# Narrowing spread over 19 units, late products moved, and a straight last block in an attention-and-SwiGLU kernel

## Chip, cores and metric

One core of one Trainium2 chip. The metric is the device time of one execution, in microseconds; the kernel before takes about 323.4. "Span" is the time from the first to the last instruction of a profiled execution; it is some 1.7 us shorter than the device time.

## The reference

```python
# attention: q, k, v are (4, 4, 1088, 32); S1, S2 are (8, 32)
def phi(x):                                        # 8 x 8 = 64 features
    a = einsum('rd,bhsd->bhsr', S1, x); b = einsum('rd,bhsd->bhsr', S2, x)
    return einsum('bhsi,bhsj->bhsij', a, b).reshape(..., 64)
kv = einsum('bhsf,bhsd->bhfd', phi(k), v);  z = sum(phi(k), axis=2)
attn = (phi(q) @ kv) / (phi(q) . z + 1e-6)
x = attn.transpose(0, 2, 1, 3).reshape(4352, 128)
# SwiGLU: w_gate, w_val (128, 1536), w_out (1536, 128)
g = x @ w_gate
out = (g * sigmoid(g) * (x @ w_val)) @ w_out
```

All inputs arrive as float64. The kernel reads them as pairs of 32-bit words and makes fp32 of them on the chip: this is the "narrowing".

## The kernel before: what the change and the argument touch

Tokens stand in 12 blocks (three per batch: 384, 384, 320), d_ff in 12 chunks of 128. One **unit** is a block and a chunk: a gate product and a value product on TensorE into two PSUM banks, silu on ScalarE, a product on VectorE. A **down** product accumulates the hidden tile times w_out. While the first batch's units run, the weights are still being narrowed, piece by piece (3 chunks, 384 columns), in three parts with a `yield` between them:

```python
def narrow(dst, raw, shape):
    ...
    # part one, VectorE: exponent field, mantissa field
    nc.vector.tensor_scalar(e[:], hi, 0x7FF00000, None, op0=ALU.bitwise_and)
    nc.vector.tensor_scalar(m[:], hi, 0xFFFFF, 0x100000, op0=ALU.bitwise_and, op1=ALU.bitwise_or)
    yield
    # part two, ScalarE: rebias, scale
    nc.scalar.activation(e[:], e[:], AF.Relu, bias=rebias[: shape[0], :], scale=8.0)
    nc.scalar.activation(f, m[:], AF.Copy, scale=2.0**-20)
    yield
    # part three, VectorE (two SBUF inputs each), then GpSimd
    nc.vector.scalar_tensor_tensor(out=e[:], in0=hi, scalar=-(1 << 31), in1=e[:], op0=ALU.bitwise_and, op1=ALU.bitwise_or)
    nc.vector.scalar_tensor_tensor(out=f, in0=lo, scalar=2.0**-52, in1=f, op0=ALU.mult, op1=ALU.add)
    mul = nc.vector if first else nc.gpsimd
    mul.tensor_tensor(out=dst, in0=f, in1=e[:].bitcast(FP32), op=ALU.mult)
    if not first:
        load_next()
    yield

def unit(i, j, late=False):
    g, u = bank(), bank()                      # banks in turn, four of them
    ...                                        # two matmuls, then silu into sg
    if late:                                   # six early units: VectorE has no time
        nc.scalar.copy(hj[:, 0:n], u[:, 0:n])
        lates.append((hj[:, 0:n], sg[:, 0:n]))
    else:
        nc.vector.tensor_tensor(out=hj[:, 0:n], in0=sg[:, 0:n], in1=u[:, 0:n], op=ALU.mult)

def catch_up():                                # the late product
    o, sg = lates.pop(0)
    nc.gpsimd.tensor_tensor(out=o, in0=o, in1=sg, op=ALU.mult)
...
parts = {0: both(3, *w), 1: both(3, *w), 2: both(3, "wg"), 4: both(3, "wv"),
         6: both(4, *w), 7: both(4, *w), 8: both(4, "wg"), 10: both(4, "wv"),
         12: [("wo", 0), ("wo", 1)], 13: [("wo", 0), ("wo", 1), ("wo", 2)], ...}
for z, (i, j) in enumerate(seq):               # units 0, 1, 2, ... of this stage
    unit(i, j)
    for p in parts.get(z, ()):
        part(*p)
    if z in (4, 10, 16, 24, 25, 26):
        catch_up()
    ...
    if z >= 17:
        down()
```

A block's result is transposed by VectorE and stored by four stores, one per 32 output columns. The very last block (320 tokens) uses two queues.

## Time and profile before

| | us |
|---|---|
| device time, median of 3 | 323.42 |
| span of the profile | 321.45 |
| unit 0's first gate product, first down product | 28.06, 52.91 |
| stage between them | 24.85 |
| end of the last matmul; from there to the end ("tail") | 316.98; 4.47 |

The numbers in rows of the timeline are start and length in us. The first 28 us load inputs and do the first batch's attention.

### The profile page before, as it was taken

How to read it: one execution, taken by the hardware profiler on the slowest of the kernel's cores; microseconds unless marked ns; L12 is line 12 of the kernel's file. 1: busy time of each engine (PE TensorE's matmuls, PEld its weight loads, DVE VectorE, ACT ScalarE, POOL GpSimd, SP SyncE). 2: the span in 40 equal slices, each digit the busy share in tenths (PEclk: the TensorE clock that was granted, in tenths of full speed). 3: DMA queues.
4: the chain of work that ended last, by engine and by line, in shares of the span. 5: the costliest groups of instructions: out<-in, count | busy, mean ns of one | idle time of the engine just before them, and what ended most of it. 6: DMA issues, size and time to landing. Idle time of an engine off the chain costs nothing.

```text
span 321.5 us, 5554 instructions
## 1 busy us (share of the span) xinstructions
PE 312.6 (97%) x2276; PEld 189.9 (59%) x2276; DVE 156.7 (49%) x330; ACT 99.0 (31%) x227; POOL 37.6 (12%) x53
## 2 busy tenths in 40 slices
PE   8889999999999999999999999999999999999994
PEld 6545555656556665555666656555667655556672
DVE  4887888653466522544643543354544332322331
ACT  3467555322121222322322322323222222222220
POOL 2322333173000140000000060000000000000000
PEclk9999999999999999999999999999999999999998
DMA  7543580204041201100210100000010100100101
GB/s 203 156 150 100 157 248 0 71 0 96 1 96 22 69 17 55 27 0 2 31 65 0 22 2 0 14 12 2 0 27 0 20 0 2 26 0 0 24 2 20
DMA packets 25017, 13.99 MB, mean 44 GB/s; under 512 B 18848, under 2 KB 23072, under 8 KB 24992
## 3 DMA queue, kind: packets, MB, share of 16 engines
q1 hardware_dynamic: 24304, 13.56, 16.5%
q8 instruction: 18, 0.29, 0.4%
q10 hardware_dynamic: 688, 0.08, 0.2%
q14 instruction: 7, 0.06, 0.1%
HBM read 11.41 MB, written 2.23 MB: 42 GB/s over the span
## 4 chain that ended last, share of the span: by engine, by line
PE 89%; DVE 5%; ACT 2%; issue 1%; DMA 1%; POOL 0%; DVEq 0%
PE bank L511 50%; PE bank L539 28%; PE a L348 2%; PE a L398 2%; PE b L348 1%; PE bank L194 1%; PE a L304 1%; ACT exp L221 1%; DVE exp L216 1%; DMA raw<-in_moe_w_out_dram 1%; PE b L398 1%; PE a L273 1%; PE b L327 1%; PE bank L316 1%; ACT man L222 0%
## 5 line engine op out<-in xcount | busy, mean ns | idle before, releaser
L525 DVE TENSOR_TENSOR hj<-sg,bank 128x384 f32<-128x384 f32 (+1 forms) x138 | 72.7, 529 | 122.6 <-PE bank L511 117.8
L517 ACT ACTIVATE sg<-bank 128x384 f32<-128x384 f32 (+1 forms) x144 | 67.8, 473 | 167.1 <-PE bank L511 165.5
L511 PE MATMUL bank<-xT,wg 128*128 128x384 f32 (+1 forms) x288 | 114.1, 478 | 2.3 <-POOL wg L232 1.1
L511 PE MATMUL bank<-xT,wv 128*128 128x384 f32 (+1 forms) x288 | 111.9, 470 | 0.3 <-DVE hj L525 0.3
L539 PE MATMUL bank<-hj,wo 128*128 128x384 f32 (+1 forms) x288 | 109.1, 471 | 0.1
L511 PEld LDWEIGHTS bank<-xT,wv 128*128 128x128 f32 x288 | 54.0, 190 | 35.2 <-DVE hj L525 3.6
L511 PEld LDWEIGHTS bank<-xT,wg 128*128 128x128 f32 x288 | 52.5, 190 | 36.8 <-issue 3.9
L539 PEld LDWEIGHTS bank<-hj,wo 128*128 128x128 f32 x288 | 54.0, 190 | 33.0 <-issue 2.4
L445 POOL TENSOR_TENSOR zs<-phk 128x1024 f32<-128x1024 f32 x3 | 7.1, 2352 | 107.1 <-PE bank L511 106.0
L376 DVE TENSOR_TENSOR phq<-a,qb 128x384 f32<-128x384 f32 (+1 forms) x11 | 5.8, 531 | 10.7 <-ACT qb L362 10.7
L362 ACT COPY qb<-a 128x384 f32<-128x384 f32 (+1 forms) x11 | 5.1, 462 | 15.0 <-PE b L348 8.6
L348 PE MATMUL b<-qT,sq 32*64 32x192 f32 (+1 forms) x176 | 9.2, 324 | 0.0
L348 PE MATMUL a<-qT,sq 32*64 32x192 f32 (+1 forms) x176 | 9.2, 324 | 0.0
L221 ACT ACTIVATE exp<-exp,rebias 128x384 int32<-128x384 int32 (+3 forms) x15 | 8.3, 550 | 2.8 <-DVE exp L216 2.0
L419 DVE STREAM_TRANSPOSE dT<-a 128x384 f32<-128x384 f32 (+1 forms) x8 | 4.4, 550 | 7.8 <-PE a L398 7.8
L362 ACT COPY qb<-b 128x384 f32<-128x384 f32 (+1 forms) x11 | 5.1, 464 | 9.7 <-PE b L348 6.4
L224 DVE SCALAR_TENSOR_TENSOR exp<-raw,exp 128x384 int32<-128x384 int32 (+2 forms) x14 | 7.4, 532 | 0.9 <-ACT exp L221 0.9
L348 PEld LDWEIGHTS a<-qT,sq 32*64 32x64 f32 x176 | 5.5, 131 | 3.9 <-issue 3.0
L376 DVE TENSOR_TENSOR phq<-b,qb 128x384 f32<-128x384 f32 (+1 forms) x11 | 5.8, 527 | 4.2 <-ACT qb L362 4.2
L555 DVE STREAM_TRANSPOSE o<-bank 128x384 f32<-128x384 f32 (+1 forms) x12 | 6.7, 561 | 2.2 <-PE bank L539 1.8
L232 POOL TENSOR_TENSOR wg<-man,exp 128x384 f32<-128x384 f32 (+2 forms) x5 | 4.6, 928 | 21.1 <-DVE man L228 21.1
L228 DVE SCALAR_TENSOR_TENSOR man<-raw,man 128x384 f32<-128x384 uint32 (+2 forms) x14 | 6.9, 493 | 0.0
(93 smaller groups left out, 164.4 us busy)
## 6 DMA issues: line engine op xcount, KB each, us to landing
kld<-in_k_dram SPq DMA_DIRECT2D x4, 544.0 KB, 4.7
vld<-in_v_dram SPq DMA_DIRECT2D x12, 144.0 KB, 4.0
qld<-in_q_dram SPq DMA_DIRECT2D x3, 544.0 KB, 3.8
raw<-in_moe_w_out_dram SPq DMA_DIRECT2D x4, 384.0 KB, 3.2
out_dram<-o SPq DMA_DIRECT2D x32, 48.0 KB, 1.8
raw<-in_moe_w_gate_dram SPq DMA_DIRECT2D x3, 384.0 KB, 3.2
raw<-in_moe_w_val_dram SPq DMA_DIRECT2D x3, 384.0 KB, 3.4
out_dram<-o SPq DMA_DIRECT2D x14, 40.0 KB, 1.7
```

Source lines behind the costliest of these rows:

```text
L221: nc.scalar.activation(e[:], e[:], AF.Relu, bias=rebias[: shape[0], :], scale=8.0)
L224: nc.vector.scalar_tensor_tensor(out=e[:], in0=hi, scalar=-(1 << 31), in1=e[:], op0=ALU.bitwise_and, op1=ALU.bitwise_or,)
L228: nc.vector.scalar_tensor_tensor(out=f, in0=lo, scalar=2.0**-52, in1=f, op0=ALU.mult, op1=ALU.add)
L348: nc.tensor.matmul(parts[g][F * half : F * half + F, t, 0:w], sq[r, t, :, :].rearrange("p i j -> p (i j)"), qT[r, x0 : x0 + n, half, :], s ...
L362: nc.scalar.copy(qb[:, :, 0:w], both[:, :, 1, 0:w])
L376: nc.vector.tensor_tensor(out=phq[:, 2 * pr : 2 * pr + 2, 0:w], in0=both[:, :, 0, 0:w], in1=qb[:, :, 0:w], op=ALU.mult,)
L398: nc.tensor.matmul(halves(nd[t])[half][32 * h : 32 * h + 32, 0:w], kvz[t][r, 32 * h : 32 * h + 32], phq[r, h, 0:w], start=True, stop=True,)
L445: add = lambda o, a, b: nc.gpsimd.tensor_tensor(out=o, in0=a, in1=b, op=ALU.add)
L511: nc.tensor.matmul(o[:, 0:n], w[:, j, :], xT[:, t0 : t0 + n], start=True, stop=True)
L517: nc.scalar.activation(sg[:, 0:n], g[:, 0:n], AF.Silu)
L525: nc.vector.tensor_tensor(out=hj[:, 0:n], in0=sg[:, 0:n], in1=u[:, 0:n], op=ALU.mult)
L539: nc.tensor.matmul(acc[i][:, 0:n], wo[:, j, :], hidden.pop((i, j))[:, 0:n], start=(j == 0), stop=(j == NCH - 1),)
```

## The change

Its intent: never two pieces' parts on one engine in one unit; late products where GpSimd is free; and a shorter end, since the last 128 tokens leave TensorE already with tokens on partitions and need no transpose. Cut to the core:

```diff
+    LAST = len(blocks) - 2
+    SPLIT = BW - P                             # 384 - 128
@@ divide: the last block's 128 tokens get another column order
+        if t0 == blocks[LAST][0]:
+            m = SPLIT // 64
+            ys = xT[:, t0 + SPLIT : t0 + BW].rearrange("p (t x a) -> p a x t", a=2, t=32)
+            ...                                # one product becomes two
@@ down
-        n = blocks[i][1]
+        n = SPLIT if i == LAST else blocks[i][1]
+    def straight(ps, j):
+        nc.tensor.matmul(ps, hidden.pop((LAST, j))[:, SPLIT:BW], wo[:, j, :], start=(j == 0), stop=(j == NCH - 1))
@@ before the last late unit
+    for _ in range(2):
+        catch_up()
     unit(1, 2, late=True)
@@ the stage
-    parts = { ... }
+    parts = {}
+    for z, p in enumerate(both(3, *w) + both(4, *w) + [("wo", i) for i in range(4)]):
+        z += z // 2 * 3
+        for at in (z, z + 1, z + 2):
+            parts.setdefault(at, []).append(p)
-        if z in (4, 10, 16, 24, 25, 26):
+        if z in (16, 24, 25, 26):
             catch_up()
-        if z == 2:
+        if z == 6:
             load_k(1)
@@ the end
-            unit(3 * b + z // NCH, z % NCH)
+            i, j = z // NCH, z % NCH
+            unit(3 * b + ((0, 2, 1)[i] if b == B - 1 else i), j)
-    while todo:
-        down()
+    ps = wide("a")[:, 0, 0:D]
+    for j in range(NCH):
+        if todo and j % 4 == 0:
+            down()
+        straight(ps, j)
+    o = fpool.tile([P, D], FP32, name="o_last")
+    nc.vector.tensor_copy(o[:], ps)
+    ...
+    dst = out.rearrange("(b pp x) d -> b pp x d", pp=32, x=NX)[b, :, x0 : x0 + P // 32, :]
+    for i, queue in enumerate((nc.sync, nc.scalar)):
+        queue.dma_start(out=dst[16 * i : 16 * i + 16], in_=o[64 * i : 64 * i + 64, :])
```

## The prediction

> **What bounds the kernel now.** I read the page first, then the chain of waits, then the timeline of TensorE, VectorE and ScalarE where the chain leaves TensorE, then the timeline of the last 6 us.
>
> ```profile
> PE 312.6 (97%) x2276; PEld 189.9 (59%) x2276; DVE 156.7 (49%) x330; ACT 99.0 (31%) x227; POOL 37.6 (12%) x53
> PE   8889999999999999999999999999999999999994
> PEclk9999999999999999999999999999999999999998
> ```
>
> TensorE is the bound nearly everywhere and its clock is whole. Only three stretches can give anything: the first 20 us, a stage from 28 to 53 us, and the last slice. From 53 us on, the chain is made of TensorE pieces alone until the last matmul. The change leaves the first 20 us as they are.
>
> Busy share hides the middle stage, because one matmul's modelled duration overlaps the next. So I use pace. In the chain, where nothing waits, one unit (gate and value product, four records) costs this, for 384 and for 320 tokens:
>
> ```profile
> 104.78 1.29 PE bank L511 x4
> 154.91 1.08 PE bank L511 x4
> ```
>
> The stage from the first unit after the attention start (28.06) to the first down product (52.91) holds 18 units in the source's order: 12 of 384 and 6 of 320 tokens. At pace: 12 x 1.29 + 6 x 1.08 = 21.96 us. It took 24.85, so 2.89 us are lost; about 0.10 of it is the restart after smaller matmuls (the first pair starts 0.75 after the unit, not 0.645). **2.8 us is all that a better spread of the narrowing can win.** The view by windows, over the same stretch, shows why it is easily missed (columns: length, then busy us of PE, PEld, DVE, ACT, POOL):
>
> ```profile
> 28.06:32.84 4.78, 4.78 (x23) 2.95 (x16) 3.91 (x11) 2.77 (x6) 0.07 (x1) 1.00 0.31 80
> 32.84:40.82 7.98, 7.83 (x25) 4.23 (x24) 6.69 (x14) 4.39 (x11) 2.96 (x3) 1.00 0.61 177
> 40.82:48.97 8.15, 7.87 (x25) 4.23 (x24) 7.15 (x16) 4.57 (x11) 2.94 (x3) 1.00 0.72 226
> 48.97:52.91 3.94, 3.44 (x11) 1.47 (x9) 3.36 (x9) 1.97 (x5) 1.00 (x1) 1.00 0.00 0
> ```
>
> PE shows 0.93 us idle where 2.8 are lost. DVE is busy 21.1 of 24.85 us, below its limit: the fault is in the order, not the load. The timeline names the order:
>
> ```profile
> 31.05 0.62 ACT L221 ACTIVATE exp<-exp,rebias 128x384 int32<-128x384 int32 x1 [0.26 <-DVE exp L216]
> 31.58 0.51 ACT L222 ACTIVATE man<-man 128x384 f32<-128x384 int32 x1
> 31.99 0.60 ACT L221 ACTIVATE exp<-exp,rebias 128x384 int32<-128x384 int32 x1
> 32.50 0.51 ACT L222 ACTIVATE man<-man 128x384 f32<-128x384 int32 x1
> 32.91 0.79 ACT L517 ACTIVATE sg<-bank 128x384 f32<-128x384 f32 x2
> 33.43 0.81 PE L511 MATMUL bank<-xT,wg 128*128 128x320 f32 x2 [0.15 <-ACT sg L517]
> ```
>
> Two pieces have their ScalarE parts in one unit, 1.86 us in a row; the silu behind them frees its bank late, and the gate product two units on waits. It repeats at 40.8 and 49.0; at 51.4 a value product waits for the VectorE product. Laying the starts against the pace, I get 0.73 us (32.8 to 35.5), 1.02 (40.1 to 43.6), 0.44 (49.0) and 0.59 (51.4), together 2.78.
>
> A second fault is visible: a VectorE operation that usually takes 0.35 takes 1.09 while GpSimd runs a late product.
>
> ```profile
> 30.66 0.35 DVE L216 TENSOR_SCALAR exp<-raw 128x384 int32<-128x384 int32 x1
> 37.91 1.00 POOL L531 TENSOR_TENSOR hj<-hj,sg 128x384 f32<-128x384 f32 x1
> 38.03 1.09 DVE L216 TENSOR_SCALAR exp<-raw 128x384 int32<-128x384 int32 x1
> ```
>
> The end:
>
> ```profile
> 315.74 1.24 PE L539 MATMUL bank<-hj,wo 128*128 128x320 f32 x4
> 317.01 0.52 DVE L555 STREAM_TRANSPOSE o<-bank 128x320 f32<-128x320 f32 x1 [1.06 <-PE bank L539]
> 317.56 0.82 SPq L561 DMA_DIRECT2D out_dram<-o  x2
> 317.56 0.89 ACTq L561 DMA_DIRECT2D out_dram<-o  x2
> ```
>
> The last matmul ends at 316.98 and the span at 321.45: 4.5 us with no product in them. The trace's semaphore updates put the last landing at 320.01, 2.45 after the first issue; 1.4 us of closing follow, which the change leaves.
>
> **What the Trainium skill says.** "SBUF — State Buffer", Who interferes with whom: VectorE operations in a two-port mode (`tensor_scalar` among them), or with two SBUF inputs while GpSimd reads SBUF, exclude GpSimd for the whole instruction, and whoever comes second blocks. The trace agrees: 0.35 became 1.09 above, and products of VectorE with one PSUM input keep 0.55 us beside GpSimd. "TensorE: Matmul & The Clock Gate", LDWEIGHTS: a load costs about its columns / 1.2 GHz, so 107 ns for 128; an exposed load here delays the next record by 0.10 us. "DMA: Bandwidth & Descriptors", Specifications: below 512 B a transfer loses line rate; the last stores here are 128 B packets, about 13 ns each on their engine. No run shows 512 B stores yet.
>
> **Part by part.**
>
> *Spread.* No narrowing is removed: eight pieces of (VectorE 2 x 0.27 + 2 x 0.47 by issue distance, ScalarE 0.93, GpSimd 1.0). The order of the built program shows part one, two and three of a piece on successive units, two pieces one unit apart, then a unit or two of rest. ScalarE has 0.93 between two silus instead of 1.86. From the end of a unit's value product, its VectorE product ends about 0.7 us later, and its bank is needed after 1.94 us (units of 384) or 1.62 (320). One insertion of 0.94 us fits. Five units hold 5 x 0.47 + 2 x 1.48 = 5.3 us of VectorE against 5.4 to 6.5 of TensorE: it fits too. So most of 2.78 comes back.
>
> *Late products.* Two go before the last late unit, at about 28 to 30 us, when GpSimd has just made its last weight piece; the rest keep their count. This removes the 0.7 us blockings at 38 and 46, which are inside the sums above, not extra.
>
> *What stays.* GpSimd's product of a pair's first piece runs 1.0 us just when VectorE's third part of the second piece, with two SBUF inputs, is due. By my schedule this blocks it about 0.6, and the product after it comes 0.2 to 0.3 us too late for a 320-token unit at units 3 and 4, about 0.1 at 8 and 9, and not at all later. The two moved late products can hold up the small `tensor_scalar` of the first batch's last division (28.8), up to 0.3 of stall. I take 0.5 in all. **Gain 2.3 us.**
>
> *Last block.* The last batch's 384-token block goes last; its down products use 256 moving columns, and 12 straight ones use the hidden tile as weights and 128 columns of w_out. Removed: 12 x 2 records x 128 columns x 0.84 ns (322/384) = 2.58 us. Added: 24 records at the pace of 128-column records, which the small transposing products (line 327) show as 0.109 us on one half of the array: 2.62. Cost 0.05, I say 0.1. The block's 256 tokens are transposed and stored beside eight straight products (1.7 us): transpose 0.45, two issues per queue 0.8. They clear the queues just in time.
>
> *Tail.* VectorE's 0.52 becomes a copy of 128 columns: 0.52 less 192 cycles at about 1 ns is 0.32, gain 0.2. One issue per queue instead of two; 64 packets of 512 B each instead of 640 of 128 B. The first packet moved 0.82 after the issue, packets lasted 1.27 and the receipt 0.35. With 128 packets over 16 engines the middle term is about 0.2: 1.37 instead of 2.45, gain 1.1. **Gain of the end: 0.2 + 1.1 - 0.1 = 1.2 us.**
>
> Sum: 2.3 + 1.2 = 3.5; 323.42 - 3.5 = 319.9. I round to 320.0.
>
> **Rivals.** (1) *The wait moves to the shared port.* If each of four pairs costs 0.4 and the division 0.6, the spread gives back 2.2 and wins 0.6: 321.7. For it: the blocking seen above, and no room in the stage's first five units. Against: later units have 0.2 to 0.6 us of room. (2) *Straight products are bound by weight loads.* Load records last 190 ns; if each must end before its matmul starts, 24 x (0.19 - 0.107) = 2.0 us are added: 322.0. For it: loads start when the matmul before starts. Against: an exposed load costs only 0.10. (3) *The landing is a fixed time.* Single stores of 48 KB land in 1.8; then the tail wins 0.2 + 0.65 and the time is 320.2. (4) *All works*: 2.78 + 1.3 = 4.1, 319.3.
>
> **Range and chances.** 319.3 and about 321.5 are the ends that one rival alone gives; both (1) and (2) together would give about 323.7. I set 319.1 to 321.5. Two per cent are 6.5 us, more than all losses named; so faster 0.02, within 2% 0.97, slower 0.01.
>
> **What would show it.** Units 0 to 17 take 22.0 to 22.6 us from the first gate product to the first down product; no gate product waits for a silu behind two ScalarE parts; no first part lasts 1.09; the third parts of second pieces last up to 1.1. At the end straight records follow each other at 0.107 to 0.12 us, and from the last matmul to the end of the span there are 3.1 to 3.5 us. I am wrong if the stage keeps over 1.5 us of loss, if straight records stand 0.15 us or more apart, or if the tail stays over 4 us.

## The result and the profile after

321.96 us, median of 4 (321.65 to 322.47), against 323.51 for the kernel before in the same rounds (4 runs). Ratio 0.9953, 95% interval 0.9935 to 0.997. A ratio is the mean of one kernel's runs over the mean of the other's of the same rounds, so it is not quite the ratio of the medians. The gain is 1.55 us where 3.5 were forecast, and the time lies 0.46 us above the range.

| us | before | after | difference | forecast |
|---|---|---|---|---|
| stage, unit 0 to first down product | 24.85 | 23.46 | -1.39 | -2.3 |
| unit 0 to end of last matmul | 288.92 | 287.72 | -1.20 | -2.2 |
| tail | 4.47 | 4.15 | -0.32 | -1.3 |

The second row less the first, +0.19, holds the straight products and the rest of TensorE's work. The page of the kernel after shows no new bound, and in the timeline the ScalarE parts no longer stand in pairs. But the stage still loses 1.5 us against its 21.96 at pace, and the timeline of its first loss says how (VectorE, GpSimd and TensorE rows):

```profile
33.58 0.55 DVE L231 SCALAR_TENSOR_TENSOR man<-raw,man 128x384 f32<-128x384 uint32 x1
34.05 0.48 DVE L533 TENSOR_TENSOR hj<-sg,bank 128x320 f32<-128x320 f32 x1
34.21 1.00 POOL L235 TENSOR_TENSOR wg<-man,exp 128x384 f32<-128x384 f32 x1 [4.17 <-DVE man L231]
34.44 1.18 DVE L227 SCALAR_TENSOR_TENSOR exp<-raw,exp 128x384 int32<-128x384 int32 x1
35.55 0.55 DVE L231 SCALAR_TENSOR_TENSOR man<-raw,man 128x384 f32<-128x384 uint32 x1
36.01 0.87 DVE L533 TENSOR_TENSOR hj<-sg,bank 128x320 f32<-128x320 f32 x2
36.54 0.91 PE L519 MATMUL bank<-xT,wv 128*128 128x384 f32 x2 [0.47 <-DVE hj L533]
```

The first piece of a pair ends at 34.1; GpSimd starts its product; the second piece's third part, 0.55 us when free, lasts 1.18 beside it; the unit's product behind it comes late, and the value product two units on, unit 6's, waits. Against the pace this costs 0.74 us, 0.10 of it the restart after the wait. The same happens at unit 11 (0.31). (The expectations below call these the stalls at units 5 and 10.) The third loss, at the first down product, has a late product in it:

```profile
49.58 1.13 POOL L539 TENSOR_TENSOR hj<-hj,sg 128x384 f32<-128x384 f32 x1
49.76 1.16 DVE L220 TENSOR_SCALAR man<-raw 128x384 int32<-128x384 int32 x1
50.84 0.54 DVE L533 TENSOR_TENSOR hj<-sg,bank 128x384 f32<-128x384 f32 x1
51.52 0.89 PE L547 MATMUL bank<-hj,wo 128*128 128x384 f32 x2 [0.21 <-DVE hj L533]
```

That late product was written at unit 16, but nothing gates GpSimd: it runs when its own queue lets it. Inside the stage 0.38 us are lost (the expectations below say 0.46). With 0.10 of restart at unit 0 the three make up the 1.5.

The end, again from the timeline:

```profile
313.84 1.95 PE L561 MATMUL a<-wo,hj 128*128 128x128 f32 x16
315.82 0.29 DVE L767 COPY o_last<-a 128x128 f32<-128x128 f32 x1 [1.33 <-PE a L561]
316.14 0.67 SPq L772 DMA_DIRECT2D out_dram<-o_last  x1
316.14 0.64 ACTq L772 DMA_DIRECT2D out_dram<-o_last  x1
```

The 16 straight records follow each other at 0.112 us ((1.95 - 0.27) / 15, the last lasting 0.27): cheap, as forecast. The copy takes 0.29 where the transpose took 0.52. But a single store takes 0.65 us to issue where the first of the old stores took 0.32. By the trace's packets and semaphore updates the two queues' first packets move 1.29 and 1.56 us after the issue (0.82 before), the packets are through in 0.25 us each, and the last landing is 2.19 after the issue, against 2.45 before for two stores per queue. From that landing to the end of the span there are 1.60 us, where there were 1.44 before.

### The profile page after: what moved, and what is told of

It is laid out like the page before. It is cut to its first block, busy times and chain, and to the rows that moved or that the text cites. A ratio compares the mean times of both kernels' runs of the same rounds, so it can differ in the third digit from the quotient of the medians.

```text
span 319.9 us, 5604 instructions
## 1 busy us (share of the span) xinstructions
PE 312.2 (98%) x2300; PEld 193.7 (61%) x2300; DVE 157.8 (49%) x332; ACT 99.0 (31%) x227; POOL 37.6 (12%) x53
## 4 chain that ended last, share of the span: by engine, by line
PE 88%; DVE 7%; issue 2%; ACT 1%; POOL 0%; DVEq 0%
PE bank L519 49%; PE bank L547 27%; DVE hj L533 2%; PE a L351 2%; PE a L401 2%; PE b L351 1%; PE bank L197 1%; PE a L307 1%; DVE exp L227 1%; PE a L561 1%; DVE man L231 1%; PE b L401 1%; PE a L276 1%; DVE exp L219 1%; ACT exp L224 1%
## 5 line engine op out<-in xcount | busy, mean ns | idle before, releaser
L547 PE MATMUL bank<-hj,wo 128*128 128x384 f32 (+2 forms) x288 | 106.8, 462 | 0.3 <-DVE hj L533 0.2
L227 DVE SCALAR_TENSOR_TENSOR exp<-raw,exp 128x384 int32<-128x384 int32 (+2 forms) x14 | 8.6, 618 | 0.9 <-ACT exp L224 0.9
L575 DVE STREAM_TRANSPOSE o<-bank 128x384 f32<-128x384 f32 (+2 forms) x12 | 6.6, 549 | 2.7 <-PE bank L547 2.3
L225 ACT ACTIVATE man<-man 128x384 f32<-128x384 int32 (+3 forms) x15 | 6.7, 450 | 0.5 <-DVE man L220 0.5
```

The lines of the kernel that those rows point to most:

```text
L547: nc.tensor.matmul(acc[i][:, 0:n], wo[:, j, :], hidden[i, j][:, 0:n], start=(j == 0), stop=(j == NCH - 1),)
```

## The experiments

All kernels have the reference's result but two, which are marked. In the table, "stage" and "tail" are as above, "to last" is unit 0 to the end of the last matmul; all three from the profile.

| run | what | stage | to last | tail | ratio (95%) |
|---|---|---|---|---|---|
| before | | 24.85 | 288.92 | 4.47 | 1 |
| after | | 23.46 | 287.72 | 4.15 | 0.9953 (0.9935-0.997) |
| e1_spread | spread only | 24.46 | 288.61 | 4.47 | 0.9996 (0.9983-1.001) |
| e5_late_only | late products only | 23.70 | 287.76 | 4.49 | 0.9983 (0.9964-1.0002) |
| e2_spread_late | both | 23.48 | 287.61 | 4.47 | 0.9952 (0.994-0.9964) |
| e3_tail | new end only | 24.84 | 289.02 | 4.12 | 0.9989 (0.9976-1.0001) |
| e4_after | all, again | 23.48 | 287.73 | 4.13 | 0.9965 (0.9951-0.9979) |
| e10_no_product | no GpSimd products (wrong result) | 22.19 | 286.37 | 4.20 | - |
| e13_early | late products earlier | 23.08 | 287.20 | 3.86 | 0.9933 (0.992-0.9946) |
| e12_early_odd | and third parts apart | 22.65 | 286.84 | 3.87 | 0.992 (0.9906-0.9934) |
| e14_rows | and last rows at one distance | 22.66 | 286.86 | 3.95 | 0.9926 (0.9913-0.994) |

**The parts alone.** Three kernels, each the kernel before with a part of the change, and the change again:

```diff
 e1_spread:       the new parts table, load_k(1) at unit 6; catch_up as before (4, 10, 16, 24, 25, 26)
 e2_spread_late:  e1_spread, two catch_up() before unit(1, 2, late=True), then (16, 24, 25, 26)
 e3_tail:         the changed kernel with the stage of before
```

> Only the narrowing's new order (and the later loads of the next batch); the late products stay where they were. Theory (the change's parts act on separate stretches and add up): units 0 to 17 take about 23.5 to 24.2 us instead of 24.85, the span is 0.7 to 1.3 us shorter. Rival (moving the late products is what paid): this run is within 0.3 us of before, since the late products still run beside the first parts.

> Narrowing's new order and the moved late products, with the old end. Theory: all of the stage's gain, 1.4 us (units 0 to 17 in 23.5 us as in the changed kernel), tail of 4.5 us as before. Rival (the new end carries the gain): only 0.3 to 0.8 us faster than before.

> Only the new end: last block's 128 tokens by straight products, stored on two queues. Theory: last matmul about 0.15 us later than before (24 records at 0.112 instead of 0.107), tail 4.15 instead of 4.47, in all 0.1 to 0.2 us faster, that is: nothing. My prediction's sizing would have it 1.2 us faster.

> The changed kernel again, on the same chip as its parts. Theory: 1.5 us faster than before, the sum of the second and third run within 0.3 us; and the profile shows again the three stalls of 0.3 to 0.7 us in units 5 to 17 and an issue of about 0.65 us for each last store. If the spread of its four times (0.8 us) comes from the last stores' landing, this profile's landing differs from 2.2 us in the same sense as its span.

The stages and tails add up: e2_spread_late has all of the stage's gain and the old tail, e3_tail the old stage and the new tail. By e3_tail the new end costs TensorE 0.10 us (289.02 against 288.92) and wins 0.35 in the tail. The scatter of the whole times (321.7 to 323.0 in e4_after) is not the last stores' landing: tail and stage of e4_after are those of the first profile within 0.02 us. It is unit 0's start, 29.43 there and 28.06 in the first profile. I did not trace that to one load.

e1_spread is the surprise: the spread alone wins only 0.39 us in its stage, and its whole time cannot be told from that of before, as the rival had it. Its timeline shows the late product of unit 4 beside a first part:

```profile
38.24 1.12 POOL L531 TENSOR_TENSOR hj<-hj,sg 128x384 f32<-128x384 f32 x1
38.42 1.15 DVE L217 TENSOR_SCALAR man<-raw 128x384 int32<-128x384 int32 x1
```

**The late products alone.** The kernel before with only `catch_up` moved:

```diff
+    for _ in range(2):
+        catch_up()
     unit(1, 2, late=True)
...
-        if z in (4, 10, 16, 24, 25, 26):
+        if z in (16, 24, 25, 26):
```

> The kernel before with two late products moved ahead of the last late unit, nothing else. Theory (the shared port: a late product of 1.0 us beside VectorE's two-port first parts costs up to 0.75 there): the two first parts of 1.09 us at 38 and 46 fall to 0.35, and the stage from unit 0 to the first down product shrinks from 24.84 to about 24.3; the silu waits at 32.8, 40.8 and 49.0 stay because the two ScalarE parts still stand together. Rival (moving them pays by itself all that the spread run lacked): 23.9 or less.

The stage falls to 23.70: the rival's figure, not the theory's. Moving two GpSimd instructions wins 1.15 us by itself, where the whole change wins 1.39. This rests on the stage of one profile, for the whole time (ratio 0.9983) cannot quite be told from that of before; but kernels with the same stage code agree in the stage within 0.03 us (after, e2, e4, e7, e9 and e11: 23.45 to 23.48), wherever unit 0 starts. The timeline shows why it is more than the 0.75 us of one blocking:

```profile
38.97 0.35 DVE L216 TENSOR_SCALAR exp<-raw 128x384 int32<-128x384 int32 x1
39.46 0.61 ACT L221 ACTIVATE exp<-exp,rebias 128x384 int32<-128x384 int32 x1
41.30 0.80 ACT L517 ACTIVATE sg<-bank 128x384 f32<-128x384 f32 x2
41.88 0.75 PE L511 MATMUL bank<-xT,wg 128*128 128x320 f32 x2
```

The two ScalarE parts still stand together ahead of the silu, and yet the gate product at 41.88 shows no wait. In the kernel before, the first parts came 0.7 us late, so ScalarE began its two parts late; this, as much as there being two, put the silu behind its time.

That holds for two of the four losses only. Laid against the pace, those of e5_late_only are 0.87, 0.34, 0 and 0.43 us, where the kernel before had 0.73, 1.02, 0.44 and 0.59. The first, which has no late product ahead of it, is as large as before, and there the gate product does wait for the silu behind two ScalarE parts:

```profile
33.85 0.80 ACT L517 ACTIVATE sg<-bank 128x384 f32<-128x384 f32 x2
34.37 0.81 PE L511 MATMUL bank<-xT,wg 128*128 128x320 f32 x2 [0.28 <-ACT sg L517]
```

The spread does away with these waits but puts third parts beside GpSimd's products instead; so on top of the moved late products it wins only 0.24 (23.70 to 23.46).

**Is it the shared port?** GpSimd's product of the spread pieces replaced by something that reads no SBUF (wrong result):

```diff
-        mul.tensor_tensor(out=dst, in0=f, in1=e[:].bitcast(FP32), op=ALU.mult)
+        if late_piece: nc.gpsimd.memset(dst, 0.01)      # the eight spread pieces
```

> Wrong result on purpose: in the changed kernel the GpSimd product of the eight spread pieces is replaced by a memset of the same tile, which reads nothing from SBUF. Theory (the remaining stalls at units 5 and 10 are VectorE's third parts blocked by GpSimd's product through the shared port): the third parts of 1.1 to 1.2 us fall to 0.55, the stalls of 0.74 and 0.31 us go, the one at the first down product (0.46, behind a late product of GpSimd) may stay; stage 22.2 to 22.6 us instead of 23.46. Rival (VectorE is simply full there, or ScalarE is late): stage stays at 23.2 or more.

This did not test it: the memsets wait for nothing, six of the eight ran in one burst from 30.0 to 32.2 us, and they and the late product behind them (32.14) held up VectorE's first parts there, so the stage grew to 25.95:

```profile
30.80 1.59 DVE L219 TENSOR_SCALAR exp<-raw 128x384 int32<-128x384 int32 x1
32.31 1.85 DVE L220 TENSOR_SCALAR man<-raw 128x384 int32<-128x384 int32 x1
```

The next form leaves the eight products out and sets their tiles once at the start (wrong result again); its end differs too, and is read apart:

```diff
+    nc.gpsimd.memset(wg[:, 6:NCH, :], 0.01); nc.gpsimd.memset(wv[:, 6:NCH, :], 0.01); nc.gpsimd.memset(wo[:], 0.01)
-        mul.tensor_tensor(...)
+        if not late_piece: mul.tensor_tensor(...)
@@ end
+    for a in range(4):                                  # packets of 128 B, 128 rows each
+        queue = nc.scalar if a % 2 else nc.sync
+        queue.dma_start(out=dst[:, :, 32 * a : 32 * a + 32], in_=o[:, 32 * a : 32 * a + 32])
```

> Wrong result on purpose. The write-only form ran all its memsets at once at 30 us and held up VectorE there, so here GpSimd's products of the eight spread pieces are left out altogether and their tiles are set once in the first microseconds. The late product of unit 16 then runs at 30 us, beside a first part. Theory (remaining stalls come from GpSimd's products and late product at the shared port): third parts all last 0.55 us, the stalls at units 5, 10 and at the first down product go, at most 0.3 us of stall near unit 2; stage 22.1 to 22.5 us instead of 23.46. Rival (VectorE full): above 23. The end is also changed, apart from this: the last 128 tokens stored in four stores of 128 rows of 128 B. If packets of 512 B make the generator slow, issues fall to 0.35 and 0.46 and the first packet comes at 0.8; if rows that lie one per partition do, issues stay at 0.65.

The stage takes 22.19 us: of the 1.5 us lost, 0.1 of restart and 0.13 more are left. The view of the tile `exp` in the window from 30 (28 in this run) us gives min/median/max in ns; first the changed kernel, then this one:

```profile
L227 DVE SCALAR_TENSOR_TENSOR exp<-raw,exp x7: 551/559/1178, 33.1 to 52.4; 128x384 int32<-128x384 int32 x7
```

```profile
L231 DVE SCALAR_TENSOR_TENSOR exp<-raw,exp x8: 542/552/553, 33.5 to 53.4; 128x384 int32<-128x384 int32 x8
```

No third part is slow without GpSimd's products, and VectorE, with the same instructions, has time enough. So the stage's remaining loss, 1.3 of the 1.5 us, is GpSimd beside VectorE: shown. That it is a shared port is not shown by this run; it fits that products with a PSUM input are not slowed beside GpSimd. What this run takes away with the blocking is GpSimd's latency too, but weights were not waited for in the changed kernel's stage.

**What the end waits for.** Three forms of the last store on top of the changed kernel:

```diff
 e7_apart:     block's stores all on SP;  nc.scalar.dma_start(out=dst, in_=o[:, :])
 e9_quarters:  for a in range(4): (sync, scalar in turn).dma_start(out=dst[8*a : 8*a+8], in_=o[32*a : 32*a+32, :])
 e11_xmajor:   as e7_apart, tokens in the usual order (no split in divide): dst is "b x pp d"
```

> The 256-token stores all on SP, and the last 128 tokens in one store on the otherwise idle ScalarE queue. Theory A (the last store's first packet is late because its queue still has the stores before it in flight): issue and first packet come back to 0.35 and 0.8 us. Theory B (the shape of 16 x 4 rows of 512 B costs the descriptor generator more): issue stays at 0.65 or grows with 128 rows to about 1.2, first packet at 1.3 us or later, tail 4.1 to 4.7.

> The last 128 tokens in four stores of 32 rows of 512 B, two on each queue. If the cost of an issue grows with its rows, each issue takes about 0.35, the first packet comes at 0.8 and the last landing at about 1.7 to 1.9 after the first issue: tail 3.7 to 3.9 instead of 4.13. If it is fixed for this shape, two issues of 0.65 follow each other and the tail grows to 4.7.

> As the single last store on the ScalarE queue, but with the last 128 tokens in the usual order, so that 32 partitions in a row lie 17 KB apart in the output and four groups of them follow (no split of the last division's product). If the order of rows in the output is what costs, issue falls from 0.64 to about 0.35 and the first packet from 1.29 to 0.8, tail 3.4; if not, 0.65, 1.3 and a tail of 3.9 as in the single store.

The timeline rows of the last stores of e7_apart, e9_quarters, e10_no_product and e11_xmajor, in this order:

```profile
316.85 0.64 ACTq L771 DMA_DIRECT2D out_dram<-o_last  x1
```

```profile
317.41 1.56 SPq L773 DMA_DIRECT2D out_dram<-o_last  x2
```

```profile
315.16 1.29 SPq L781 DMA_DIRECT2D out_dram<-o_last  x2
```

```profile
316.76 0.65 ACTq L765 DMA_DIRECT2D out_dram<-o_last  x1
```

An idle queue does not help (e7_apart: 0.64, first packet 1.29 after the issue). Rows do not count: 128 in one store 0.64, 64 0.65, 32 0.80 and 0.71. Nor does the packet: 128 B in e10_no_product, 0.65, first packet 1.30. In e11_xmajor the same issue and first packet; there the packets then took 0.91 us to move instead of 0.36, and the tail grew to 4.41, which nothing of mine had foreseen. The traces show why: the store of e7_apart ends with 16 marks of 4 B, that of e11_xmajor with 4, and the times of its packets sum to 4 times their span against 10. So I read its 128 packets as going over four DMA engines and not sixteen: 32 of 27 ns in a row are 0.87 us. In e9_quarters issues of 0.80 and 0.71 do follow each other, the last landing is 3.00 after the first issue, and the tail is 4.82. Theory B of e7_apart held for issue and first packet, but its tail, 3.88, is below the 4.1 to 4.7 that it named. The single store is the better end: it lands 2.00 after the issue, not 2.19, because with two queues the second queue's first packet came 0.27 later than the first's.

One thing was common to all of these: the rows lie one per partition and, in the output, at two distances (four neighbours, then a jump of 34 rows; in e11_xmajor 32 rows 34 apart, four times). Two distances alone are not enough: the old stores have them too, with ten rows of 128 B on each partition, and issue in 0.32 with the first packet at 0.82. The last run, on top of e12_early_odd below, stores 32 rows at one distance each time:

```diff
+    dst = out.rearrange("(b pp x) d -> b x pp d", pp=32, x=NX)[b, x0 : x0 + P // 32, :, :]
+    for x in range(P // 32):
+        queue = nc.scalar if x % 2 else nc.sync
+        queue.dma_start(out=dst[x], in_=o[32 * x : 32 * x + 32, :])
```

> The version with shifted third parts, and the end changed once more: the last 128 tokens in the usual order and stored in four stores of 32 rows, each store's rows at one even distance in the output (two stores on each queue).[...] Theory (rows in two levels, groups of four neighbours, are what costs a store 0.65 us of issue and 1.3 to its first packet): issues of 0.32 and 0.46, first packet at 0.8, last landing 1.7 after the first issue, tail 3.5 to 3.6. Rival (any store with one row per partition costs that, whatever its row distances): two issues of 0.65 or more follow each other, tail 4.6 to 4.9.

```profile
315.94 0.80 SPq L770 DMA_DIRECT2D out_dram<-o_last  x2
315.95 0.85 ACTq L770 DMA_DIRECT2D out_dram<-o_last  x2
```

Two stores now issue in the time of little more than one (0.33 and 0.42 on SP), with the first packet 0.83 after the issue. Against e9_quarters, which has the same four stores of 32 packets of 512 B on the same queues, the stores differ in the rows' pattern (and in the end marks that come with it, 16 a store against 8). So two distances, for rows that lie one per partition, are what cost 0.65 and 1.3: the theory holds in this form. It wins nothing, however: the second pair's packets start 0.91 after their own issue, the last landing is 2.07 after the first issue, and the tail is 3.95 instead of the 3.5 to 3.6 that I expected.

**A version that beats both.** Late products earlier still (two after the third late unit, two where the change has them, none at unit 16), the single last store, and, in e12_early_odd, the third part of each pair's second piece one unit later:

```diff
     unit(0, 2, late=True)
+    for _ in range(2):
+        catch_up()
-        if z in (16, 24, 25, 26):
+        if z in (25, 26):
@@ e12_early_odd only
+        odd = z % 2
         z += z // 2 * 3
-        for at in (z, z + 1, z + 2):
+        for at in (z, z + 1, z + 2 + odd):
```

> The same without the third parts' shift: tells what the early late products give alone. Theory: the stall at the first down product (0.46) goes, those at units 5 and 10 stay (0.74 and 0.31); stage 23.0, tail 3.9; 2.3 us faster than before.

> A version that should beat both: single last store, two late products earlier (after the third late unit), the next two where the change has its two, none at unit 16, and the third part of each pair's second piece one unit later, so that it does not stand right behind GpSimd's product of the first. Theory (shared port): the three stalls (0.74, 0.31, 0.46) fall to 0.3 together, stage about 22.4, tail 3.9; 2.9 us faster than before, 1.3 faster than the changed kernel. Rival (one unit later only moves the collision to the next pair's first parts): stage 23 or more.

e13_early loses its stall at the first down product and keeps the other two, as expected (23.08). In e12_early_odd those go as well, but the stage is 22.65, between theory and rival: 0.6 us remain beside the 0.1 of restart. Its timeline shows the cure: two unit products, which have one PSUM input and do not mind GpSimd, now stand where the blocked third part stood.

```profile
34.32 0.91 DVE L533 TENSOR_TENSOR hj<-sg,bank 128x320 f32<-128x320 f32 x2
35.14 0.76 DVE L227 SCALAR_TENSOR_TENSOR exp<-raw,exp 128x384 int32<-128x384 int32 x1
36.69 0.97 DVE L219 TENSOR_SCALAR exp<-raw 128x384 int32<-128x384 int32 x1
```

The collision does move on, as the rival said: the next first part lasts 0.97. In the first pair it does so where there is slack. In the fourth pair it does not: a first part beside GpSimd's product (48.90 to 49.90) lasts 0.91, and 0.30 of the 0.6 us are lost again at the first down product:

```profile
49.20 0.91 DVE L219 TENSOR_SCALAR exp<-raw 128x384 int32<-128x384 int32 x1
50.99 0.89 PE L547 MATMUL bank<-hj,wo 128*128 128x384 f32 x2
```

The whole takes 320.66 us (median of 6) against 323.33: ratio 0.992. Its interval lies below both intervals of the changed kernel, which was measured in other rounds; it overlaps that of e13_early, so what the shift adds is read from the stage alone (0.43).

## Why the prediction was wrong

- **The bound, the pace and the size of the loss** were right: without GpSimd's products the stage takes 22.19, close to the 21.96 at pace plus 0.1 of restart. 2.8 us was indeed all that could be won there.
- **"I take 0.5 in all. Gain 2.3 us" failed**: the residue was 1.5 (0.1 of it the restart at unit 0), the gain 1.39. The mechanism of rival 1 was named, and the blocking's length (0.6) was right to a few hundredths (1.18 less 0.55). What failed is the slack that the term built on it takes for granted, "0.2 to 0.3 us too late for a 320-token unit at units 3 and 4, about 0.1 at 8 and 9, and not at all later". The units were right, the sizes not: 0.74 behind the product of unit 4 and 0.31 behind that of unit 9, a restart of 0.10 in each, which the term had left out. In e10_no_product, with no third part blocked, the same value product of unit 6 still comes 0.04 late (0.14 with its restart): the first pair has no slack, so the whole blocking is paid. I had let each pair start with VectorE on time. In the trace the first unit's product starts at 30.35 behind the division; that the lateness runs on from there is my reading, and no run tests it.
- **"the rest keep their count"**: I counted the late product written at unit 16 and never asked when GpSimd would run it. Free to go, it met a first part at 49.8 (1.16, though "no first part lasts 1.09" was forecast), and that is the third stall, 0.38; e13_early removes it by moving that product.
- **"This removes the 0.7 us blockings at 38 and 46, which are inside the sums above, not extra"**: true of the sum, wrong about the cause. Alone, moving the late products wins 1.15 and the spread 0.39. I gave the stalls to the pile of ScalarE parts because the trace named ScalarE as the releaser; for the losses at 41 and 49 us the releaser's own lateness came from VectorE, blocked by GpSimd. For the first it did not.
- **"the middle term is about 0.2 ... gain 1.1" failed**, though not in the middle term. The packets took 0.25 and the receipt 0.38, near the forecast of 0.2 and 0.35. The term taken over unchanged, "the first packet moved 0.82 after the issue", was 1.29 and 1.56 for the new stores. e14_rows ties it to rows, one per partition, at two distances. The 1.4 us of closing, taken as left alone, were 1.60 instead of 1.44, and what sets them is open. So the tail gained 0.23 + 0.26 - 0.16 = 0.33, and at 4.15 it stayed over the 4 us that the prediction had named as a sign of being wrong.
- **The straight products** (0.1) and **the copy** (0.2) came as sized: 0.10 by e3_tail, and 0.23. Rivals 2 and 3 fell: records stand 0.112 apart, and the landing is not a fixed time, since it moved with the rows' pattern.
- The range's upper end, 321.5, lay below what the prediction itself gave for rival 1 alone (321.7; its terms sum to 321.6) and for rival 2 alone (322.0), so it had no room for them. Part of rival 1 came and the landing went the worse way too, and the sum is outside. (Rival 3's terms sum to 320.4, not 320.2; nothing rests on it.)

## What to carry to other kernels

When the trace says that an engine waited for B, look at what made B late, and test by moving that one thing alone: alone, moving two instructions on an idle engine won 1.15 us, and the rewritten schedule 0.39. When parts are spread, check what stands beside each GpSimd instruction: in these traces VectorE products with a PSUM input kept their 0.45 to 0.56 us there, while first parts went from 0.35 to as much as 1.16 and third parts with two SBUF inputs from 0.55 to 1.18. And a store's time to its first packet belongs to its pattern, so it may not be carried over from another store.

## What the Trainium skill lacked or had wrong

- "DMA: Bandwidth & Descriptors", Latency and other measured facts, gives about 0.6 us to the first byte for DMAs issued from these two engines, without a pattern and without saying from when it counts. Here it was 0.82 to 0.83 from the start of the issue for the old stores and for rows, one per partition, at one distance, and 1.28 to 1.30 (with 0.64 to 0.65 of issue) for such rows at two distances, on the first queue to move. Counted from the end of the issue it was 0.50 to 0.51 and 0.63 to 0.66, so most of the difference is the issue itself. Apart from e9_quarters with its longer issues, the number of rows and the packet's size made no difference.
- The same page, Specifications, asks for 512 B for line rate. A packet of 512 B took 28 ns and one of 128 B 13, so it agrees about the rate; but for a last store of 64 KB the rate is not what is waited for (0.25 of 2.19 us).
- "SBUF — State Buffer", Who interferes with whom, was right in kind (third parts 0.55 free, 1.1 to 1.2 beside a GpSimd product). It does not say what a run of GpSimd instructions does: one first part of 0.35 us lasted 1.59 beside a burst of memsets (e6_write_only), while in the changed kernel one of 0.17 lasted only 0.32 beside two products in a row.
